# Token gathers one round earlier in the expert stage, and one weight conversion ahead of the first block's copy

## The chip, the cores and the metric

The kernel runs on one core of a Trainium2 chip. The metric is the device time of one execution in microseconds. A core has five engines with an instruction stream each: TensorE (PE in the rows; PEld is its weight load), VectorE (DVE), ScalarE (ACT), GpSimd (POOL) and SyncE (SP), which here only starts transfers. Every stream runs in order: an instruction that waits for a semaphore holds back whatever stands behind it in the same stream. POOL and ACT start transfers too (POOLq, ACTq); the transfers of all three run on the core's 16 DMA engines.

## The reference

Three layers follow each other. An xLSTM-like attention yields 3072 tokens of 320 values. A layer of 8 experts sends each token to the expert with the highest gate logit. A gated feed-forward layer ends it. The change is in the second:

```python
logits = x @ w_gate
e_idx = np.argmax(logits, axis=1)
probs = softmax(logits); gate_w = probs[arange(N), e_idx]
eom = 1 / (1 + exp(-(x @ w_output_gate)))
for e in range(8):
    mask = e_idx == e
    h = relu(x[mask] @ w1[e])          # 320 -> 1024
    out[mask] = gate_w[mask] * eom[mask, e] * (h @ w2[e])   # 1024 -> 320
```

## The kernel before, in words

The program is written by hand, and each engine's stream holds its instructions in the order in which the code issues them. Weights and activations are split into two float16 halves (high and low), so that a product is three matmuls.

**Routing** (`route`) sorts the tokens by expert into blocks of 128 slots, of which 28 always run. `IDX` holds the token of each slot. Behind it come the conversions of the second half of `w2`: `hi` on ACT (L881, 128x1280) and `lo` on DVE (L888). Three raw pieces are parked in the destination of another piece, so the `hi` of piece 4 may write only after the `lo` of piece 6 has read its slot, and that of piece 5 after the `lo` of piece 4. `moe_fetch` starts the gathers of blocks 0 and 1 and turns block 0 on TensorE (`xflip`, L1111), with a copy to `xt` on ACT (L1113).

**The rounds** (`moe`): round `j` runs `up(j)` (16 matmuls of 512 columns, L1143, then ReLU on ACT, the low half on DVE, and two DMA transposes `hT<-h` on SP, L1151) and `down(j-2)` (24 matmuls of 320 columns, L1175). A block's tokens reach `up(j)` in two steps:

- `gather(j)` on POOL (L1095): 128 rows of 1,536 bytes from `XD` in HBM into `xg`. There are two `xg` buffers, so `gather(j+2)` waits until `xpose(j)` has read `xg` of block `j`.
- `xpose(j)` on SP (L1103): a DMA transpose of `xg` into `xt`.

`cgather(j)` on POOL (L1087) fetches the 128 output factors of block `j` into `CG`. `evac(j)` on ACT (L1185) reads them two rounds after the fetch; the first fetch waits for the factors to be written by `coefs`.

**Beside the rounds** 16 jobs (`ffn_jobs`) convert a third of the next layer's weights. A job loads 384 KB on SP into one of four `stg` buffers (L1313), DVE and ACT convert it over four steps, and POOL stores 160 KB into `UWS` (L1341). The load of job `k+4` takes the buffer of job `k`, and so waits on SP until the store of job `k` has landed. `due` says in which round each step runs, and `tick(j, 0)` issues those of part 0 in the middle of `up(j)` and `tick(j, 1)` those of part 1 at the round's end. Loads stand in rounds 2, 3, 4, 5, 6, 8, 9, 10, 11, 12, 14 to 18 and 20, stores in rounds 6 to 10, 12 to 16, 18 to 22 and 24. For three pairs the store of job `k` and the load of job `k+4` fall into the same round: rounds 6, 12 and 18.

SP's order in a round is `xpose(j+1)`, the two `hT` transposes of `up(j)`, the job's load, and then `xpose(j+2)`. In round 23 POOL also starts `fetch(0)`, the first rows of the next layer (L1368), which ACT squares in round 24 (L1383) and TensorE turns at the end of the stage (L1422).

Of the kernel before, what the change touches and what calls it, by code (L numbers as in the profile page):

```python
# [32 lines left out]
NJ = NBLK - 3  # L33
# [41 lines left out]
class Net:  # L75
# [821 lines left out]
    def route(self):  # L897
# [3 lines left out]
        def t(block, n, shape, dt=F32):  # L901

            if block not in blocks:
                if block < 2:
                    b = self.M.tile([128, 2, 4, 128], F16, tag="hT", bufs=5, name="rt").rearrange("p s k c -> p (s k c)")
                else:
                    b = self.M.tile([128, 2, 512], F16, tag="h", bufs=3, name="rt").rearrange("p s f -> p (s f)")
                blocks[block] = [b, 0]
            b, o = blocks[block]
            k = 1  # L910
            for d in shape[1:]:
                k *= d
            w = k * (1 if dt == F16 else 2)
            assert o + w <= 1024
            blocks[block][1] = o + w
            a = b[0 : shape[0], o : o + w]
            a = a if dt == F16 else a.bitcast(dt)
            if len(shape) == 3:
                a = a.rearrange("p (a b) -> p a b", b=shape[2])
            return a  # L920
# [16 lines left out]
        def warm(k):  # L937
            e = P.tile([128, 512], F32, tag="dn", bufs=2, name="warm")
            for _ in range(k):
                nc.tensor.matmul(e, self.id[:, 0:64].bitcast(BF), self.W1[:, 0:512].bitcast(BF), start=True, stop=True)  # L940
# [56 lines left out]
            s = slice(64 * two, 64 * two + 64)  # L997
            nc.vector.tensor_scalar(self.IDX[s], pi[two][s, 0:NBLK], float(NT // 2), None, ALU.add)
        warm(WM[4])
        self.moe_fetch()  # L1000
        ce = t(4, "ce", [1, NBLK, NE], F16)
        nc.vector.scalar_tensor_tensor(
            out=ce, in0=iota[0:1, 0:NBLK].unsqueeze(2).to_broadcast([1, NBLK, NE]), scalar=128.0,
# [8 lines left out]
        w2[0][1]()  # L1012
        w2.append(self.w2load(7))
        w2[4][1]()
        w2[5][0]()
        w2[1][1]()

# [74 lines left out]
    def gather(self, j, xg=None):  # L1092
        if xg is None:
            xg = self.M0.tile([128, 2 * DX], F16, tag="xg", bufs=2, name="xg")
        self.nc.gpsimd.indirect_dma_start(  # L1095
            out=xg, out_offset=None, in_=self.XD,
            in_offset=bass.IndirectOffsetOnAxis(ap=self.IDX[:, j : j + 1], axis=0),
        )
        self.T[j] = dict(xg=xg)

    def xpose(self, j):
        xt = self.M0.tile([128, 6, 128], F16, tag="xt", bufs=2, name="xt")
        self.nc.sync.dma_start_transpose(out=xt, in_=self.T[j]["xg"])  # L1103
        self.T[j]["xt"] = xt
# [7 lines left out]
        xt = self.T[j]["xt"] = self.M0.tile([128, 6, 128], F16, tag="xt", bufs=2, name="xt")  # L1112
        nc.scalar.activation(xt, px, AF.Copy)  # L1113

    def moe_fetch(self):
        self.T, self.X = {}, {}
        self.gather(0)
        self.gather(1)
        self.xflip(0)

    def moe(self):
        nc, M, P = self.nc, self.M, self.P
        gather, xpose = self.gather, self.xpose
# [3 lines left out]
        def up(j, mid=None):  # L1127
            t = T[j]
            e = nc.tensor.value_load(self.EOFF[0:1, j : j + 1], min_val=0, max_val=NE - 1)
            t["e"] = e  # L1130
            o1 = nc.tensor.snap(e * (5 * F1))
            t["hT"] = []
            if j >= NJ:
                own = spare.bitcast(F16)[:, 0:2048].rearrange("p (f s k c) -> p f s k c", f=2, s=2, k=4)
            for f in range(2):
                h = M.tile([128, 2, 512], F16, tag="h", bufs=3, name="h")
                if j < NJ:
                    hT = M.tile([128, 2, 4, 128], F16, tag="hT", bufs=5, name="hT")
                else:
                    hT = own[:, f]  # L1140
                ps = P.tile([128, 512], F32, tag="up", bufs=4, name="ups")
                for n, (kx, kw) in enumerate(UP):
                    nc.tensor.matmul(  # L1143
                        ps, t["xt"][:, kx], self.W1[:, ds(o1 + (kw * F1 + f * 512), 512)],
                        start=(n == 0), stop=(n == 7),
                    )
                nc.scalar.activation(h[:, 0], ps, AF.Relu)  # L1147
                nc.vector.scalar_tensor_tensor(  # L1148
                    out=h[:, 1], in0=ps, scalar=0.0, in1=h[:, 0], op0=ALU.max, op1=ALU.subtract
                )  # L1150
                nc.sync.dma_start_transpose(  # L1151
                    out=hT.rearrange("p s k c -> p (s k) c"), in_=h.rearrange("p s f -> p (s f)")
                )
                t["hT"].append(hT)
                if f == 0 and mid:
                    mid()

        def down(j, mid={}):
            t = T[j]
            oa = nc.tensor.snap(t["e"] * (2 * KA * DM))  # L1160
            ob = nc.tensor.snap(t["e"] * (2 * KB * DM))
            ps = P.tile([128, 512], F32, tag="dn", bufs=2, name="dps")
            n = 0
            for k in range(8):
                if k in mid:
                    mid[k]()
                if k < KA:
                    W, o, kk, nk = self.W2A, oa, k, KA
                else:
                    W, o, kk, nk = self.W2B, ob, k - KA, KB  # L1170
                hi = W[:, ds(o + kk * DM, DM)]
                lo = W[:, ds(o + (nk + kk) * DM, DM)]
                hT = t["hT"][k // 4]
                for l, r in ((0, hi), (1, hi), (0, lo)):
                    nc.tensor.matmul(ps[:, 0:DM], hT[:, l, k % 4], r, start=(n == 0), stop=(n == 23))  # L1175
                    n += 1
            t["dn"] = ps

        def evac(j):
            ps = T[j]["dn"]  # L1180
            if j not in (NJ - 3, NJ - 1):
                y = self.LG.rearrange("p i e -> p (i e)")[:, 0:YC]
            else:
                y = self.M0.tile([128, DX], F32, tag="xg", bufs=2, name="yl")[:, 0:YC]
            nc.scalar.activation(y[:, 0:DM], ps[:, 0:DM], AF.Copy, scale=self.CG[:, j : j + 1])  # L1185
            nc.scalar.activation(y[:, DM:YC].bitcast(I32), self.TOK[:, j : j + 1], AF.Copy)
            nc.scalar.dma_start(self.YD[128 * j : 128 * j + 128], y)
            T.pop(j)
# [11 lines left out]
        def tick(j, part):  # L1200
            for step in due.pop((j - 2, part), []):
                step()
# [3 lines left out]
        gather(3)  # L1206
        gather(4)
        for j in range(NJ):
            if 5 <= j + 2 < NJ:
                gather(j + 2)  # L1210
            if 2 <= j and j + 1 < NJ:
                xpose(j + 1)
            up(j, lambda: tick(j, 0) if j else self.xflip(1))
            if j == 0:
                w2[5][1]()
                w2[2][1]()
                scr = lambda: M.tile([128, 2, 512], F16, tag="h", bufs=3, name="scr").rearrange(
                    "p s f -> p (s f)"
                ).bitcast(F32)
            elif j == 1:  # L1220
                w2[7][0]()
                w2[3][1]()
                w2[7][1]()
                self.weigh(scr())
            elif j == 2:
                down(0)
                self.coefs(scr())
                self.order(scr())
            if j in (8, 10, 12):
                b = NJ + (j - 8) // 2  # L1230
                nc.gpsimd.dma_start(
                    self.YD[128 * b : 128 * b + 128].rearrange("p (s c) -> p s c", s=3),
                    self.zero.unsqueeze(1).to_broadcast([128, 3, YC // 3]),
                )
            if j == 2:
                self.cgather(0)
            if j >= 2:
                self.cgather(j - 1)
            if j > LAG:
                evac(j - LAG - 1)  # L1240
            if j > LAG:
                down(j - LAG)
            if j == FJ[0]:
                self.fetch(0, first=True)
            elif j == FJ[1]:
                self.squares(0, range(4))
                self.norm1(0)
                self.tokens(0)
            elif j == FJ[2]:
                for m in range(4):  # L1250
                    self.norm2(0, m)
            tick(j, 1)
# [428 lines left out]
```

## Time and profile before

| | us |
|---|---|
| three runs of the kernel | 798.79, 808.02, 815.62 |
| median | 808.02 |
| the profiled execution | 794.23 |
| its span, first to last instruction | 792.4 |
| expert stage in that span (first `up` matmul to the last `down`) | 211 to 417 |

The profiled execution is 14 us below the median of the runs shown and 4.6 us below the lowest. Times in the rows are microseconds from the span's start. A timeline row reads: start, duration, engine, line, operation, output<-input, count, and in brackets the idle time of that engine before it with what the profile takes for the releaser. The profile puts a wait for several semaphores down to the one that it saw last; on POOL several rows name DVE where the instruction in the program waits for DMAs alone.

### The profile page before, as it was taken

To read this page: it belongs to the slowest core of one execution; us is meant where nothing else is said; L and a number is where in the kernel's file an instruction comes from. 1 tells how busy PE (TensorE), PEld (TensorE's weight loads), DVE (VectorE), ACT (ScalarE), POOL (GpSimd) and SP (SyncE) were. 2 spreads that over 40 slices of the span, in tenths; PEclk is the share of its full clock that TensorE was granted. 3 is DMA by queue.
4 is the path that set the end of the run, shared out by engine and by line. 5 is a ranking of instruction groups with operands and counts; after the bars stand their busy time and mean duration, and the time that the engine had idled before them with its cause. 6 is when DMAs were issued, how large, how long until landed. Compare 5 with 4: busy or idle time off the path is not lost. (4 is left out here: it accounts for less than half of the span.)

```text
span 792.4 us, 15458 instructions
## 1 busy us (share of the span) xinstructions
PE 758.9 (96%) x5292; PEld 483.0 (61%) x5294; DVE 434.1 (55%) x894; ACT 358.9 (45%) x777; POOL 375.2 (47%) x458
## 2 busy tenths in 40 slices
PE   8899999998798999999989999999999999999997
PEld 8799998986344555555554444444565665644664
DVE  7678988897764646564315776778712112133110
ACT  4578878783532333332436665655422132133110
POOL 2557877883322424234516875765634242233221
PEclk9999999999898999999999999999999999999999
DMA  6587877864669999999965332231131021000000
GB/s 186 169 282 227 278 238 245 268 208 163 206 137 198 212 236 231 238 224 200 191 144 201 99 81 69 76 82 50 51 74 43 26 55 27 26 0 1 13 22 34
DMA packets 131429, 109.21 MB, mean 138 GB/s; under 512 B 104535, under 2 KB 111375, under 8 KB 131353
## 3 DMA queue, kind: packets, MB, share of 16 engines
q1 hardware_dynamic: 120905, 86.64, 43.5%
q0 software_dynamic: 6368, 16.94, 7.4%
q10 hardware_dynamic: 4080, 4.62, 1.8%
q8 instruction: 48, 0.79, 0.4%
q14 instruction: 28, 0.23, 0.1%
HBM read 67.59 MB, written 16.82 MB: 107 GB/s over the span
## 5 line engine op out<-in xcount | busy, mean ns | idle before, releaser
L1518 PE MATMUL gv<-XT,UW 128*128 128x512 f16 x1152 | 249.8, 379 | 1.6 <-DMA XT<-xr 1.6
L1518 PEld LDWEIGHTS <-UW 128*128 128x128 f16 x1152 | 112.6, 98 | 136.9 <-DMA XT<-xr 2.1
L1528 DVE SCALAR_TENSOR_TENSOR u<-th,gv 128x512 f32<-128x512 f32 x72 | 49.4, 686 | 155.6 <-ACT th L1522 153.9
L1534 POOL TENSOR_TENSOR h<-u,h 128x512 f16<-128x512 f32 x72 | 84.8, 1180 | 105.2 <-ACT h L1533 104.8
L1551 PE MATMUL do<-DW,h 128*128 128x320 f16 x864 | 118.5, 299 | 0.9 <-POOL DW L1472 0.9
L1143 PE MATMUL ups<-W,xt 128*128 x448 | 103.7, 385 | 10.2 <-DMA xt<-xg 6.4
L1551 PEld LDWEIGHTS <-h 128*128 128x128 f16 x864 | 84.5, 98 | 34.9 <-issue 1.2
L1533 ACT ACTIVATE h<-u 128x512 f16<-128x512 f32 x72 | 45.3, 629 | 112.7 <-DVE u L1529 112.7
L1147 ACT ACTIVATE h<-ups 128x512 f16<-128x512 f32 x56 | 33.3, 596 | 115.3 <-PE ups L1143 107.8
L1175 PEld LDWEIGHTS <-hT 128*128 128x128 f16 x672 | 65.6, 98 | 31.7 <-issue 2.3
L1148 DVE SCALAR_TENSOR_TENSOR h<-ups,h 128x512 f16<-128x512 f32 x56 | 38.4, 691 | 81.9 <-ACT h L1147 81.5
L1143 PEld LDWEIGHTS <-xt 128*128 128x128 f16 x448 | 44.3, 99 | 62.2 <-DMA xt<-xg 9.4
L1095 POOL DMA_INDIRECT xg<-XD,IDX x28 | 29.7, 1060 | 85.2 <-DMA xt<-xg 38.8
L1556 POOL DMA_INDIRECT out_dram<-os,TKN x24 | 23.5, 977 | 80.3 <-ACT os L1554 76.7
L1529 DVE SCALAR_TENSOR_TENSOR u<-u,gv 128x512 f32<-128x512 f32 x72 | 49.5, 688 | 14.5 <-PE gv L1518 10.2
L485 PE MATMUL S<-QK 104*128 104x128 f32 x384 | 51.6, 278 | 1.8 <-DMA QK<-in_pqk_dram 1.8
L1175 PE MATMUL dps<-W2A,hT 128*128 x336 | 50.5, 299 | 2.1 <-ACTq L1258 2.1
L485 PEld LDWEIGHTS S<-QK 104*128 104x128 f32 x384 | 50.0, 194 | 3.5 <-issue 2.7
L541 PEld LDWEIGHTS Y<-t,D 128*128 128x128 f32 x352 | 49.2, 192 | 3.4
L541 PE MATMUL Y<-t,D 128*128 128x41 f32 x352 | 51.2, 248 | 0.0
L1554 ACT ACTIVATE os<-do 128x320 f32<-128x320 f32 x24 | 10.5, 437 | 88.8 <-PE do L1551 80.7
L1175 PE MATMUL dps<-W2B,hT 128*128 x336 | 50.6, 299 | 0.0
(280 smaller groups left out, 1161.5 us busy)
## 6 DMA issues: line engine op xcount, KB each, us to landing
t<-in_pk_dram SPq DMA_DIRECT2D x22, 484.0 KB
QK<-in_pqk_dram SPq DMA_DIRECT2D x48, 160.0 KB
stg<-in_wu_dram SPq DMA_DIRECT2D x16, 384.0 KB
stg<-in_w_dram SPq DMA_DIRECT2D x9, 640.0 KB
XD<-xr SPq DMA_DIRECT2D x24, 192.0 KB
YD<-LG ACTq DMA_DIRECT2D x26, 160.5 KB
stg<-in_w_dram SPq DMA_DIRECT2D x8, 512.0 KB
wraw<-in_wo_dram SPq DMA_DIRECT2D x12, 320.0 KB
```

What stands on the lines that cost most here:

```text
L485: nc.tensor.matmul(ps[:, i * L : (i + 1) * L], t["kz"][:, j, i], t["t1"][:, i], start=True, stop=True)
L541: nc.tensor.matmul(t["Y"][:, hp, 41 * hf : 41 * hf + 41], t["D"][hf][:, hp * L : (hp + 1) * L], t["vv"][:, 4 * hf + hp], start=False, stop ...
L1143: nc.tensor.matmul(ps, t["xt"][:, kx], self.W1[:, ds(o1 + (kw * F1 + f * 512), 512)], start=(n == 0), stop=(n == 7),)
L1147: nc.scalar.activation(h[:, 0], ps, AF.Relu)
L1148: nc.vector.scalar_tensor_tensor(out=h[:, 1], in0=ps, scalar=0.0, in1=h[:, 0], op0=ALU.max, op1=ALU.subtract)
L1175: nc.tensor.matmul(ps[:, 0:DM], hT[:, l, k % 4], r, start=(n == 0), stop=(n == 23))
L1518: nc.tensor.matmul(ps, UW[:, f, gv, kw], xt[:, :, 3 * hl + kx], start=(a == 0), stop=(a == 7))
L1528: nc.vector.scalar_tensor_tensor(out=u, in0=th, scalar=1.0, in1=pg, op0=ALU.add, op1=ALU.mult)
L1529: nc.vector.scalar_tensor_tensor(out=u, in0=u, scalar=1.0 / (XN * WSC) ** 2, in1=pv, op0=ALU.mult, op1=ALU.mult)
L1533: nc.scalar.activation(hh, u, AF.Copy)
L1534: nc.gpsimd.tensor_tensor(hl, u, hh, ALU.subtract)
L1551: nc.tensor.matmul(ps[:, 0:DM], l[:, s], DW[:, f, w], start=(a == 0), stop=(a == 3 * NF - 1))
```

## The change

Three edits. `moe_fetch` is dissolved: its two gathers stay where they were, and its `xflip(0)` moves behind the `hi` of piece 4, so that ACT converts this piece before it copies block 0. In `moe` the line that gathers now stands behind `xpose(j+1)`, and it gathers block `j+3`, no more `j+2`.

```diff
@@ route
         warm(WM[4])
-        self.moe_fetch()
+        self.T, self.X = {}, {}
+        self.gather(0)
+        self.gather(1)
         ce = t(4, "ce", [1, NBLK, NE], F16)
...
         w2[6][1]()
         w2[4][0]()
         w2[0][1]()
         w2.append(self.w2load(7))
         w2[4][1]()
+        self.xflip(0)
         w2[5][0]()
         w2[1][1]()
...
-    def moe_fetch(self):
-        self.T, self.X = {}, {}
-        self.gather(0)
-        self.gather(1)
-        self.xflip(0)
@@ moe
         for j in range(NJ):
-            if 5 <= j + 2 < NJ:
-                gather(j + 2)
             if 2 <= j and j + 1 < NJ:
                 xpose(j + 1)
+            if 5 <= j + 3 < NJ:
+                gather(j + 3)
             up(j, lambda: tick(j, 0) if j else self.xflip(1))
```

**POOL, rounds 0 to 6.** `xg` is a gather (numbers grow with the block; the first row is block 4), `CG` a fetch of factors, `UWS` a job's store. Lines below the change have other numbers in the new program. Before:

```order
L1095 DMA xg_3202<-XD_81,IDX_69 128x768
L1087 DMA CG_67<-CD_83,IDX_69 128x1 x2
L1095 DMA xg_3393<-XD_81,IDX_69 128x768
L1087 DMA CG_67<-CD_83,IDX_69 128x1
L1095 DMA xg_3465<-XD_81,IDX_69 128x768
L1087 DMA CG_67<-CD_83,IDX_69 128x1
L1095 DMA xg_3542<-XD_81,IDX_69 128x768
L1087 DMA CG_67<-CD_83,IDX_69 128x1
L1095 DMA xg_3625<-XD_81,IDX_69 128x768
L1341 DMA UWS_87<-stg_3391 128x640
```

Now:

```order
L1098 DMA xg_3202<-XD_81,IDX_69 128x768
L1098 DMA xg_3312<-XD_81,IDX_69 128x768
L1090 DMA CG_67<-CD_83,IDX_69 128x1 x2
L1098 DMA xg_3397<-XD_81,IDX_69 128x768
L1090 DMA CG_67<-CD_83,IDX_69 128x1
L1098 DMA xg_3469<-XD_81,IDX_69 128x768
L1090 DMA CG_67<-CD_83,IDX_69 128x1
L1098 DMA xg_3546<-XD_81,IDX_69 128x768
L1090 DMA CG_67<-CD_83,IDX_69 128x1
L1098 DMA xg_3629<-XD_81,IDX_69 128x768
L1338 DMA UWS_87<-stg_3393 128x640
```

The gather of block 5 now stands ahead of the first two fetches of factors. From there on every fetch and every store has one more gather ahead of it: the store of job 0 (round 6) stood behind the gather of block 8, and stands behind that of block 9.

**ACT at the end of routing and in the first block.** `W2B` is a conversion of L881, `xt<-xpx` the copy of a block, `h<-ups` a ReLU. Before:

```order
L881 ACTIVATE W2B<-W2B 128x1280
L1113 ACTIVATE xt<-xpx 128x768
L881 ACTIVATE W2B<-W2B 128x1280 x2
L1147 ACTIVATE h<-ups 128x512
L1113 ACTIVATE xt<-xpx 128x768
```

Now:

```order
L881 ACTIVATE W2B<-W2B 128x1280 x2
L1116 ACTIVATE xt<-xpx 128x768
L881 ACTIVATE W2B<-W2B 128x1280
L1144 ACTIVATE h<-ups 128x512
L1116 ACTIVATE xt<-xpx 128x768
```

One of the two conversions that stood between the two copies now stands ahead of both. The streams of TensorE, DVE and SP keep their order.

## Rows read from the trace of the kernel before

**Rows 1.** The page, 40 slices of the span: granted TensorE clock, DMA share.

```profile
PEclk9999999999898999999999999999999999999999
DMA  6587877864669999999965332231131021000000
```

**Rows 2.** Waits of TensorE, 205 to 415: total us, times, longest.

```profile
PE ups L1143 <- DMA xt<-xg: 6.4, 5, 3.8
PE dps L1175 <- ACTq L1258: 2.1, 1, 2.1
```

**Rows 3.** Waits of POOL and of SP's queue, same stretch and columns.

```profile
POOL xg L1095 <- DMA xt<-xg: 38.8, 7, 7.4
...
SPq L1103 <- DMA xg<-XD,IDX: 1.5, 2, 0.9
```

**Rows 4.** Timeline, end of routing and first block.

```profile
210.11 0.81 ACT L1113 ACTIVATE xt<-xpx 128x768 f16<-128x768 f16 x1 [3.77 <-PE xpx L1111]
...
210.82 1.26 ACT L881 ACTIVATE W2B<-W2B 128x1280 f16<-128x1280 f32 x1
...
213.64 1.27 ACT L881 ACTIVATE W2B<-W2B 128x1280 f16<-128x1280 f32 x1 [1.56 <-DVE W2B L888]
...
216.24 7.07 PE L1143 MATMUL ups<-W,xt 128*128 x32 [1.21 <-DVE h L1148]
```

**Rows 5.** Timeline of rounds 3 to 5: transposes of blocks 4 and 5.

```profile
231.43 1.23 SPq L1103 DMA_TRANSPOSE xt<-xg  x1
...
234.55 0.95 POOL L1095 DMA_INDIRECT xg<-XD,IDX  x1 [0.30 <-issue]
...
235.39 3.61 PE L1143 MATMUL ups<-W,xt 128*128 x16 [0.25 <-DMA xt<-xg]
...
239.17 1.22 SPq L1103 DMA_TRANSPOSE xt<-xg  x1
...
246.03 6.10 PE L1143 MATMUL ups<-W,xt 128*128 x16 [3.77 <-DMA xt<-xg]
```

**Rows 6.** Stretches: busy us of the engines, granted clock, DMA share, GB/s.

```profile
238.00:244.00 6.00, 4.27 (x29) 2.62 (x27) 3.45 (x7) 1.22 (x3) 0.94 (x1) 1.00 1.04 217
244.30:251.10 6.80, 5.07 (x12) 1.88 (x13) 0.83 (x2) 1.46 (x4) 1.88 (x2) 0.50 0.84 198
...
408.00:415.00 7.00, 5.40 (x48) 4.02 (x48) 0.00 (x0) 1.67 (x6) 0.00 (x0) 1.00 0.60 177
```

**Rows 7.** Timeline of POOL: stores of rounds 6, 7 and 13, gather of round 7.

```profile
254.95 0.61 POOL L1341 DMA_DIRECT2D UWS<-stg  x1 [2.31 <-issue]
...
261.85 0.95 POOL L1095 DMA_INDIRECT xg<-XD,IDX  x1 [5.01 <-DVE stg L1335]
262.79 0.60 POOL L1341 DMA_DIRECT2D UWS<-stg  x1
...
304.54 0.59 POOL L1341 DMA_DIRECT2D UWS<-stg  x1
```

**Rows 8.** Timeline of SP's queue: loads and transposes of rounds 6 and 12.

```profile
262.04 1.42 SPq L1313 DMA_DIRECT2D stg<-in_wu_dram  x1
263.55 1.36 SPq L1103 DMA_TRANSPOSE xt<-xg  x1
...
303.65 0.53 SPq L1313 DMA_DIRECT2D stg<-in_wu_dram  x1
304.27 1.22 SPq L1103 DMA_TRANSPOSE xt<-xg  x1
```

**Rows 9.** Line L1341, the 16 stores into `UWS`, from issue to landing.

```profile
DMA to landing us min/median/max: 2.6/4.5/6.6
```

**Rows 10.** Timeline of TensorE: first matmuls of rounds 8 and 14.

```profile
269.41 3.61 PE L1143 MATMUL ups<-W,xt 128*128 x16 [0.59 <-DVE stg L1301]
...
311.49 3.61 PE L1143 MATMUL ups<-W,xt 128*128 x16 [0.92 <-DMA xt<-xg]
```

**Rows 11.** Timeline of rounds 23 to 27: last row fetch, first square, first flip.

```profile
377.56 0.97 POOL L1368 DMA_INDIRECT stg<-YD,RSLOT  x1 [0.17 <-issue]
...
385.64 0.44 ACT L1383 ACTIVATE junk<-stg 128x320 f32<-128x320 f32 x1 [0.40 <-ACT LG L1186]
...
412.55 0.50 PE L1422 MATMUL fpx<-stg 128*128 128x128 f16 x6
```

## The prediction

> **What bounds the kernel now.** I read the page's slices first. TensorE holds its full clock nearly everywhere, and in slices 10 and 12 it loses a little [rows 1]. In slices 12 to 19, the rounds of the expert stage, the DMA line is at its top. So two things are full there, and a late transfer becomes a wait of TensorE. The waits of TensorE in this stage say how much there is to win: 6.4 us for `xt<-xg` in five waits, one of 3.8 among them [rows 2]. A gather earlier helps only if transposes wait for gathers. SP's waits answer that: `xpose` (L1103) waited for `xg` twice, 1.5 us together, while the gathers (L1095) waited 38.8 us for `xt<-xg`, that is for a transpose to have read the buffer [rows 3]. **Except at the start of the stage, the gathers wait for transposes and not the other way round.** A gather that its buffer holds doesn't go out sooner because it stands sooner in POOL's stream; it only stands longer in front of what is behind it.
>
> **The change, part by part.** The sum is made on the profiled execution (794.2 us, 14 us under the median of the runs shown); I add its difference to the median.
>
> 1. *The conversion ahead of the first copy.* ACT sat idle for 3.77 us before it copied block 0, and converted piece 4 right after, 1.26 us with no wait of its own. Piece 5 then waited 1.56 us more for DVE's `lo` of piece 4, ran until 214.9, and so the copy of block 1 came late and `up(1)` waited 1.21 us [rows 4]. With piece 4 in the idle time, `lo` of piece 4 and `hi` of piece 5 move up by over a microsecond, and the copy of block 1 is in time. Bounds: -1.2 (the wait goes, and all of it reaches round 3) and +1.3 (piece 4's data comes so late that the conversion delays the copy by itself). That it ran with no wait right after the copy puts the data ahead of that. I take -0.8, two thirds of the wait, because DVE's other `lo` steps stand behind ReLU and can't all move.
>
> 2. *The gather of block 5.* Before, it stood behind the first two fetches of factors, which wait for the factors, and left at 234.55; `xpose(5)` left at 239.17 and TensorE got block 5 at 246.03 after a gap of 3.77 us [rows 5]. Now it stands ahead of those fetches, and its buffer is free once `xpose(3)` has landed. SP's wait of up to 0.9 us [rows 3] goes; I count 0.7. Its 192 KB also leave the stretch in which `xpose(5)` is on the way: at the 217 GB/s of that stretch [rows 6] some 0.9 us. So the gap falls from 3.77 to about 2.2. After the old gap the clock was at half (granted 0.50, 1.2 GHz) and 16 matmuls took 6.10 us where they take 3.61 [rows 5, 6], so 2.5 us more. A gap of 2.1 us at the end of the stage left the clock at 1.00 [rows 2, 6], which is nearer to 2.2 than 3.77 is. I take -1.6 and -2.5, together -4.1; bounds 0 and -6.3.
>
> 3. *Three stores behind one more gather.* In round 6 the store of job 0 left at 254.95. Now the gather of block 9 stands ahead of it. That gather left at 261.85 and the next store at 262.79, right behind it [rows 7]; its buffer can't be free sooner, so job 0's store takes this slot, 7.8 us later. (The row names a DVE step as the releaser; the instruction waits for DMAs alone.) Most stores can bear this, since the load that needs their buffer comes a round later. In rounds 6, 12 and 18 it comes in the same round, at 262.04 in round 6 [rows 8], before the store has even left. SP then waits at the load, and `xpose(8)` stands behind it, with the `hT` transposes of round 7. A store takes 2.6 to 6.6 us to land, median 4.5 [rows 9]. The transpose leaves 0.6 us after its load [rows 8], and a transpose behind a load took from 4.0 us to the first matmul (231.43 to 235.39 [rows 5], with little in SP's queue) to 7.2 (304.27 to 311.49 [rows 8, 10], with a full one). I take 5.0, nearer to the short one, because SP has issued nothing for over 4 us. Round 8 would start at 262.79 + 4.5 + 0.6 + 5.0 = 272.9 and not at 269.41, +3.5. For the load of round 12 the slot is 304.54 [rows 7], and round 14 starts at 314.6 and not at 311.49, +3.1. Round 18 repeats it; I take the mean, 3.3. Together +9.9. Bounds: the shortest of each (2.6 + 0.6 + 4.0) gives +0.6 and +0.2 and about 0.4, +1.2; the longest (6.6 + 0.6 + 7.2) gives 7.8, 7.4 and 7.6, +22.8.
>
>    The Trainium skill, "DMA: Bandwidth & Descriptors", section "Anatomy of one DMA — SWDGE (gpsimd) path", puts a transfer from this path at about 2.0 us plus its bytes over 436 GB/s, which is 2.4 us for such a store. By that the three waits would shrink by 2.1 us each and the sum of this step to 3.6. The rows have 4.5 in the middle, with the DMA engines full, and the sum goes by them.
>
> 4. *The clock after those gaps.* With the 0.59 and 0.92 us that rounds 8 and 14 waited already [rows 10], the three gaps come to about 4 us each, as long as the one that halved the clock [rows 5, 6]. Each halving costs 2.5 us. Taking two of three: +5.0; bounds 0 and +7.5.
>
> 5. *Edits at nothing.* The fetches of factors go out a gather later, by up to a round; `evac` reads them two rounds after, and a round is 7.0 us here ((311.49 - 269.41) / 6 [rows 10]). The other twelve loads that reuse a buffer wait for a store of an earlier round; if one of them lands at 6.6 instead of 4.5, 2 us could be lost. `fetch(0)` stands behind the gather of block 26 instead of 25, and its last row fetch moves from 377.56 by up to a round; the squares at 385.64 then end a few microseconds late and delay a ReLU of round 25 by about one, which TensorE doesn't read for two rounds, and the flips come at 412.55 only [rows 11]. Without this cover it would cost a round's 7 us.
>
> Sum: -0.8 - 4.1 + 9.9 + 5.0 = **+10.0 us**, 804 on the profiled execution and 808.0 + 10.0 = **818 us** on the median.
>
> **Rivals.**
>
> *The stores land in time, and the stage gets faster.* The mechanism is the slot of step 3: from the store's issue to the first matmul there are 269.41 - 262.79 = 6.6 us in round 6 and 7.0 in round 12 [rows 7, 10]. If landing, load and transpose together take about 7 us, near their shortest sum of 7.2, step 3 costs about 1 and step 4 nothing. What is left is -0.8 - 4.1 + 1.2 = -3.7: 804 us. For it: with SP held, the DMA engines have less to do, and a transpose without a load ahead may land sooner than any row here shows. Against it: POOL's own gather and fetch go out beside the store, and medians give 10.1. The 2.4 us for a store of the Trainium skill's page ("DMA: Bandwidth & Descriptors", the same section) would lead to this side.
>
> *Early gathers pay as a rule.* If the gathers did move, because POOL's idle time before them is DVE's as the rows say and not the buffer's, the waits of 6.4 us and the halved clock's 2.5 us would go and step 3 not arise: -0.8 - 6.4 - 2.5 = -9.7, 798 us. The 38.8 us of [rows 3] speak against it. The Trainium skill, "DMA: Bandwidth & Descriptors", section "Rules for kernel authors", says to issue a DMA early and to wait for it late; by that rule the time would come out on this side, and these rows bear it out only where the buffer is free.
>
> *Everything lands late.* Step 3 near its upper bound (about +18), three halvings (+7.5), and 4.9 gained: +20 us, 828 us. The row for it is 304.27 to 311.49, a transpose that took 7.2 us with no help from this change.
>
> *The change does nothing that shows.* Steps 2 and 3 cancel within 3 us: 808 us.
>
> **How the numbers follow.** Chances: forecast (from +4 to +16) 0.55, stores in time 0.14, early gathers pay 0.05, late landings 0.16, nothing that shows 0.10. The predicted time is the likeliest case, 818. The range takes in the stores in time at its low end and late landings at its high end, with some microseconds for the spread of the runs shown (798.79 to 815.62): 802 to 832. Two per cent, about what a measurement of this kernel can tell from no change, are 16.2 us: slower than 824.2 are the late landings and the upper edge of the forecast with a high median, 0.22; faster than 791.9 would need the early gathers and a low median, 0.03; the rest, 0.75, lies within.
>
> **What would show it.** Right: SP's load (L1310 then) waits about 4 us in rounds 6, 12 and 18, and TensorE waits 3 to 5 us for `xt<-xg` at the start of rounds 8, 14 and 20, with the granted clock at 0.5 behind some of them; the gap at round 5 is near 2 us and that at round 1 gone; the gathers from round 6 on leave at the same point of a round as before. Wrong: loads that leave on time, gathers a round sooner in time, or a gap at round 5 that stays at 3.8. If the three gaps come without a halved clock, step 4 falls and 813 is nearer.

## The result and the profile after

The changed kernel takes 807.19 us (median of 21 runs, 801.91 to 819.85), the kernel before 804.02 in as many runs beside it. The ratio is 1.0058, 95% interval 1.0035 to 1.0082: **4.7 us slower (2.8 to 6.6)**. The ratio leaves out, on both sides, the runs over 1.5% above the fastest one, so it differs a little from the 3.2 us between the medians. The forecast was +10.0 us and 818 us: the sign is right, the size about twice too large. Of the 10.8 us between 818 and 807.19, 4.0 lie in the base (808.02 from three runs, 804.02 from 21).

The profiled execution after took 813.31 us. That it lies 19 us above the one of before is for the greater part not the change: the page shows the clock below nine tenths in slices 6, 8 and 10 (counted from 0, as in the prediction), which lie ahead of the experts (they start at 225 us, in slice 11).

```profile
PEclk9999998959799999999999999999999999999999
DMA  6587877755459999999877332231221011000000
```

So only the expert stage is compared, from its first `up` matmul to the first matmul of the next layer: 206.5 us before, 211.2 after. The second profiles of the two kernels (`e6_before`, `e5_again` below) have 210.9 and 214.7: the difference is alike, but one kernel's stage varies as much from one execution to the next. The waits of that stage, of TensorE, POOL and SP's queue (total us, times, longest), which answer to [rows 2, 3]:

```profile
PE ups L1140 <- DMA xt<-xg: 9.6, 7, 2.9
...
POOL xg L1098 <- DMA xt<-xg: 54.9, 9, 14.0
POOL xg L1098 <- DMA hT<-h: 24.3, 4, 8.0
...
SPq L1310 <- DMA UWS<-stg: 11.4, 5, 4.8
SPq L1106 <- DMA xg<-XD,IDX: 1.2, 1, 1.2
```

Three things are to be seen. SP now waits for stores, 11.4 us in all; in the profile of before it did not (1.2 us, once, in `e6_before`). The gathers stand longer for their buffer (38.8 us before, 54.9 now behind the same transfer; their whole idle time is 85.2 and 115.5), as the prediction's first paragraph has it, and the gather of block 9 leaves at the same point, 0.4 us ahead of the first matmul of round 7 (0.1 before). And TensorE waits 3.2 us longer for `xt`.

Rounds 6 and 12 on the timeline: the store on POOL, the load that needs its buffer and the transpose on SP, and the first matmuls two rounds on (start, duration, engine and line; in brackets TensorE's wait):

```profile
271.28 0.61 POOL L1338 DMA_DIRECT2D UWS<-stg  x1
...
274.58 0.33 SPq L1310 DMA_DIRECT2D stg<-in_wu_dram  x1
275.00 1.95 SPq L1106 DMA_TRANSPOSE xt<-xg  x1
...
280.15 5.08 PE L1140 MATMUL ups<-W,xt 128*128 x15 [2.56 <-DMA xt<-xg]
...
316.57 0.59 POOL L1338 DMA_DIRECT2D UWS<-stg  x1
...
320.44 0.33 SPq L1310 DMA_DIRECT2D stg<-in_wu_dram  x1
320.87 1.37 SPq L1106 DMA_TRANSPOSE xt<-xg  x1
...
325.47 4.89 PE L1140 MATMUL ups<-W,xt 128*128 x16 [2.85 <-DMA xt<-xg]
```

This is step 3, link by link. The load leaves 3.30 and 3.87 us behind the store (3.43 in round 18), the transpose 0.42 later, and the matmuls 5.15 and 4.60 later (5.37). The forecast had 4.5, 0.6 and 5.0. Together 8.9 to 9.2 us instead of 10.1. TensorE waits 2.56, 2.85 and 1.98 us before rounds 8, 14 and 20, where it waited 0.59, 0.92 and 0.51 [rows 10 for the first two]: 5.4 us more, not 9.9.

Behind the first two of these gaps the clock is at half (granted 0.50, 1.2 GHz), behind the third it is not (1.00). A stretch behind the gap before round 8 (busy us of PE, PEld, DVE, ACT, POOL with counts, granted clock, DMA share, GB/s):

```profile
280.40:283.60 3.20, 3.20 (x9) 1.21 (x8) 0.00 (x0) 0.00 (x0) 2.51 (x3) 0.50 0.94 215
```

Rounds 8 and 14 then last 1.69 and 1.28 us longer than the 6.71 of a round without a wait. That is 3.0 us for step 4, not 5.0.

Round 5, which answers to [rows 5]: its transpose leaves at 251.49, and the first matmul runs at 257.29 with no wait and at full clock. Before, there were 3.77 us of wait and a halved clock.

```profile
251.49 1.33 SPq L1106 DMA_TRANSPOSE xt<-xg  x1
...
257.29 2.97 PE L1140 MATMUL ups<-W,xt 128*128 x13
```

The first block, which answers to [rows 4]: `up(1)` waits nearly as long as before (1.05 us, 1.21 before).

```profile
229.42 0.81 ACT L1116 ACTIVATE xt<-xpx 128x768 f16<-128x768 f16 x1 [1.52 <-PE ups L1140]
...
230.38 1.89 PE L1140 MATMUL ups<-W,xt 128*128 x8 [1.05 <-ACT xt L1116]
```

The copy of block 1 waits for matmuls of `up(0)`, not for ACT's conversions: there are two `xt` buffers, one holds block 2 by then, and the copy takes that of block 0, so it can't begin before `up(0)` has ended.

At the end of the stage, in round 24, ACT stands still for 5.24 us in front of a ReLU, and rounds 25 and 26 start 0.96 and 1.61 us late. That is 2.6 of the 4.8 us by which this profile's stage is longer, and the second profile of the change does not have it (0.8 us there, below). "Remote" means that the trace has no releaser.

```profile
399.65 0.60 ACT L1144 ACTIVATE h<-ups 128x512 f16<-128x512 f32 x1 [4.54 <-PE ups L1140]
...
405.48 0.60 ACT L1144 ACTIVATE h<-ups 128x512 f16<-128x512 f32 x1 [5.24 <-remote]
```

### The profile page after: what moved, and what is told of

It reads as the page before. It is cut to its first block, busy times and chain, and to the rows that moved or that the text cites. A ratio compares the mean times of both kernels' runs of the same rounds, so it can differ in the third digit from the quotient of the medians.

```text
span 811.5 us, 15452 instructions
## 1 busy us (share of the span) xinstructions
PE 770.2 (95%) x5292; PEld 492.3 (61%) x5294; DVE 434.8 (54%) x894; ACT 359.3 (44%) x777; POOL 373.9 (46%) x458
## 5 line engine op out<-in xcount | busy, mean ns | idle before, releaser
L1098 POOL DMA_INDIRECT xg<-XD,IDX x28 | 27.6, 986 | 115.5 <-DMA xt<-xg 54.9
L485 PE MATMUL S<-QK 104*128 104x128 f32 x384 | 55.4, 291 | 3.4 <-DMA QK<-in_pqk_dram 3.4
L485 PEld LDWEIGHTS S<-QK 104*128 104x128 f32 x384 | 54.1, 208 | 5.2 <-issue 4.2
L541 PEld LDWEIGHTS Y<-t,D 128*128 128x128 f32 x352 | 53.2, 206 | 4.0 <-issue 0.9
L541 PE MATMUL Y<-t,D 128*128 128x41 f32 x352 | 54.4, 259 | 0.0
L1519 ACT ACTIVATE th<-gv 128x512 f32<-128x512 f32 x72 | 42.2, 586 | 17.4 <-PE gv L1515 17.4
```

The source lines that it names most:

```text
L485: nc.tensor.matmul(ps[:, i * L : (i + 1) * L], t["kz"][:, j, i], t["t1"][:, i], start=True, stop=True)
L541: nc.tensor.matmul(t["Y"][:, hp, 41 * hf : 41 * hf + 41], t["D"][hf][:, hp * L : (hp + 1) * L], t["vv"][:, 4 * hf + hp], start=False, stop ...
L1519: nc.scalar.activation(th, pg, AF.Tanh, scale=0.5 / (XN * WSC))
```

## The experiments

All ratios are to the kernel before, run beside them. **Store theory:** the loss is what the three held loads do to the transposes behind them. **Rivals:** the loss lies in the other rounds, through POOL's other order; or there is a gain at round 5 of the forecast's size, which hides part of a larger loss.

**The three held loads alone** (`e2_stores`, the kernel before with only this):

```diff
-            if 5 <= j + 2 < NJ:
+            if 5 <= j + 2 < NJ and j not in (7, 13, 19):
                 gather(j + 2)
             if 2 <= j and j + 1 < NJ:
                 xpose(j + 1)
+            if j in (6, 12, 18):
+                gather(j + 3)
```

> The kernel before, with the gathers of blocks 9, 15 and 21 one round sooner, in rounds 6, 12 and 18, so that just the three stores whose buffer the same round's load wants stand behind a gather that waits for its buffer. Store theory: SP waits at those three loads, gaps at rounds 8, 14 and 20 grow by 1.5 to 2 us each (5.4 in the changed kernel's profile) and a halved clock adds up to 3; 5 to 9 us slower, ratio 1.006 to 1.011. As my forecast had it, 10 us for the gaps and 5 for the clock: 1.019. Rival (the stores' place is of no weight): 0.998 to 1.002.

Ratio 1.0111 (1.0053 to 1.0168), +8.9 us (4.2 to 13.4). Its waits of SP and TensorE in the stage:

```profile
SPq L1315 <- DMA UWS<-stg: 14.4, 3, 5.8
```

```profile
PE ups L1143 <- DMA xt<-xg: 15.8, 7, 4.4
```

The held loads alone make the kernel slower, by 8.9 us against the 14.9 of steps 3 and 4. Whether that is more than the whole change costs the intervals don't tell.

**The change with the store ahead of the gather** (`e3_swap`): the gather stands behind `up(j)`, in whose middle the store is issued.

```diff
-            if 5 <= j + 3 < NJ:
-                gather(j + 3)
             up(j, lambda: tick(j, 0) if j else self.xflip(1))
+            if 5 <= j + 3 < NJ:
+                gather(j + 3)
```

> The changed kernel, with the gather of block j+3 behind up(j) in place of in front of it, so that a job's store in the middle of up(j) stands ahead of the gather again; the fetches of factors stay behind it. Store theory: SP waits at no load, the gaps at rounds 8, 14 and 20 are under 1 us as in the kernel before, and the gain at round 5 stays: 5 us faster than the kernel before, ratio 0.992 to 0.996. Rival (late fetches of factors, or gathers at other times, cost what the change lost): as the changed kernel, 1.003 to 1.008.

Ratio 1.0006 (0.9964 to 1.0048).

```profile
SPq L1310 <- DMA UWS<-stg: 1.1, 1, 1.1
```

No load of rounds 6, 12 and 18 waits as in the change (1.1 us in all), and no loss is left that the interval (-2.9 to +3.8 us) could show. The gain of 5 us that I had expected from round 5 did not come: that round still waits 2.06 us.

**The conversion alone** (`e4_conv`, the kernel before with the edits in `route`).

```diff
-        self.moe_fetch()
+        self.T, self.X = {}, {}
+        self.gather(0)
+        self.gather(1)
...
         w2[4][1]()
+        self.xflip(0)
```

> The kernel before with the conversion of piece 4 ahead of the copy of block 0 alone. As forecast: the wait of 1.2 us at block 1 goes and 0.8 us come of it. From the changed kernel's trace, where this wait is 1.05 us: the copy of block 1 takes the buffer of block 0 and can't start before up(0) has ended, so 0.2 us at most. Ratio 0.998 to 1.001 either way; what tells them apart is the wait of TensorE at block 1, 0 to 0.4 us or 1.0 to 1.2.

Ratio 1.0002 (0.9961 to 1.0042), and the wait of `up(1)` is again 1.05. From the first `up` matmul to that of round 3 it is 17.0 to 17.1 us in the eight profiles with this edit and 17.2 to 17.3 in the nine without: step 1 is worth 0.2 us at most.

**Step 2.** The gather of block 5 alone, in round 2 (`e1_early5`, and profiled a second time, `e8_early5`), and the gathers of blocks 5 to 7 as in the change, with the old order from round 6 (`e7_start`). The edits on the kernel before, of `e1_early5` and of `e7_start`:

```diff
-            if 5 <= j + 2 < NJ:
+            if 6 <= j + 2 < NJ:
                 gather(j + 2)
...
+            if j == 2:
+                gather(5)
```

```diff
-            if 5 <= j + 2 < NJ:
+            if 8 <= j + 2 < NJ:
                 gather(j + 2)
...
+            if 2 <= j <= 4:
+                gather(j + 3)
```

> The kernel before, with one gather moved: that of block 5 stands ahead of the first two fetches of factors (round 2) and not behind them. All other gathers keep their round. Store theory (the change loses time only where SP is held at a load by a late store): the gap at round 5 and its halved clock go (6.4 us in the changed kernel's profile), round 4 gives 1.0 us back, no gap of 2 us or more at rounds 8, 14 and 20; 5 us faster, ratio 0.992 to 0.996. Rival (gathers at other times slow the transposes on the full DMA engines, wherever they go): the gap only moves from round 5 to a neighbour, ratio 0.998 to 1.003.

> The kernel with the gather of block 5 alone moved, for a second profile. If the early gather of block 5 doesn't touch the gap at round 5: 3 us or more again. Rival (the first profile caught a DMA stall): under 2 us.

> The gathers of blocks 5, 6 and 7 a round sooner, as in the changed kernel, and from round 5 on the order of the kernel before, so that no store stands behind one more gather. If the changed kernel's start makes the gain at round 5 (POOL held at the gather of block 7 keeps its transfers out of the stretch in which the transpose of block 5 runs): gap at round 5 under 1 us, no halved clock, 1 us back at round 4, no gaps over 2.2 us at rounds 8 and 20; ratio 0.992 to 0.996 to the kernel before. Rival (the gap at round 5 comes and goes by itself): a gap of 2 us or more, ratio 0.997 to 1.002.

`e1_early5`: ratio 0.9966 (0.9925 to 1.0008). `e7_start`: 0.9989 (0.9950 to 1.0029). Round 5 of `e7_start`, whose stream on POOL up to there is that of the change:

```profile
237.72 1.14 SPq L1315 DMA_DIRECT2D stg<-in_wu_dram  x1
238.97 1.22 SPq L1103 DMA_TRANSPOSE xt<-xg  x1
...
246.97 5.30 PE L1143 MATMUL ups<-W,xt 128*128 x16 [4.50 <-DMA xt<-xg]
```

The gap is 4.50 us, longer than before. `e1_early5` has 3.66 there, `e8_early5`, the same program, 2.12. So the same stream on POOL gives a gap of another length in each execution. The 0 us in the profile after can't be read as the change's gain.

**Both kernels profiled again** (`e5_again` the change, `e6_before` the kernel before).

> The changed kernel once more, for a second profile. If its profile shows the change and not one execution: SP waits for stores at the loads of rounds 6, 12 and 18 (11 to 15 us in all), gaps of 2 to 3.5 us at rounds 8, 14 and 20, under 1 us at round 5; rounds 25 and 26 take 6.7 to 7.7 us each. Rival (the 5 us in which ACT stood still in round 24 of the first profile belong to the change): round 25 or 26 takes over 7.5 us again, with a ReLU of round 24 late by 4 us or more.

> The kernel before once more, for a second profile, to see how far the gap at round 5 varies by itself. If that gap is made by the order of POOL's stream: 3.3 to 4.2 us again, with a halved clock. Rival (it depends on when the DMA engines happen to stall): outside of that, 2 to 3 or over 4.3.

The change: SP waits for stores again, three times and 9.6 us in all, and rounds 8, 14 and 20 wait 2.51, 0.66 and 2.33 us. The gap at round 5 is 2.74, not under 1. Two squares of the next layer wait for their rows on ACT:

```profile
SPq L1310 <- DMA UWS<-stg: 9.6, 3, 4.7
```

```profile
ACT junk L1380 <- DMA stg<-YD,RSLOT: 3.9, 2, 3.4
```

The kernel before has a gap of 4.55 at round 5 and a halved clock, and its squares wait for no row.

**The change without the three held loads** (`e9_three`, and profiled again, `e15_three_again`): only the gathers of blocks 9, 15 and 21 go back behind the store.

```diff
-            if 5 <= j + 3 < NJ:
+            if 5 <= j + 3 < NJ and j not in (6, 12, 18):
                 gather(j + 3)
             up(j, lambda: tick(j, 0) if j else self.xflip(1))
+            if j in (6, 12, 18):
+                gather(j + 3)
```

> The changed kernel, but in rounds 6, 12 and 18 alone the gather stands behind the middle of the round again, and so behind the store; all other gathers keep the place of the change. If the three held loads are the whole loss (store theory): SP waits for stores under 2 us in sum and not 11.4, the gaps at rounds 8, 14 and 20 are under 1.5 us each, and the ratio to the kernel before is 0.997 to 1.001 (799 to 803 where before has 802). Rival, the loss lies elsewhere too (later fetches of factors, later rows of the next layer): the ratio stays at 1.003 to 1.006.

> The changed kernel with the three stores ahead of the gather, profiled a second time. If its gaps at rounds 10, 14, 18 and 20 (2.8, 1.8, 1.6, 2.8 us in the first profile) follow from its order, POOL's two gathers within 3 to 5 us of each other and a transpose that then takes over 8 us, they come again at the same rounds, over 1.5 us each. If they come by chance, as the gap at round 5 does, they stand at other rounds.

Ratio 1.0049 (1.0013 to 1.0086). No load waits for a store, as expected, but by this ratio a loss stays, and the store theory as I had put it would fall: the held loads would not be all of it. The ratio is a weak witness, though, since the medians of all runs, 804.09 and 804.55 for the kernel before, show no loss. Round 8 of `e9_three` and the matmuls of round 10:

```profile
267.63 0.95 POOL L1098 DMA_INDIRECT xg<-XD,IDX  x1 [5.79 <-DVE stg L1300]
268.59 0.59 POOL L1340 DMA_DIRECT2D UWS<-stg  x1
...
270.75 1.29 POOL L1098 DMA_INDIRECT xg<-XD,IDX  x1 [0.30 <-issue]
272.04 0.59 POOL L1340 DMA_DIRECT2D UWS<-stg  x1
...
274.77 2.19 SPq L1106 DMA_TRANSPOSE xt<-xg  x1
...
283.38 0.81 PE L1140 MATMUL ups<-W,xt 128*128 x3 [2.79 <-DMA xt<-xg]
```

Two gathers and two stores leave within 4.4 us, a transpose that leaves right behind them needs 8.6 us to the matmul, and TensorE waits 2.79 us. The second profile has its large gaps at rounds 12 and 14 (3.02, 1.75), not at rounds 10, 14, 18 and 20 as the first: only round 14 comes again. So where the gaps stand does not follow from this order.

**The transposes ahead of the loads.** The transposes of blocks are what TensorE waits for, and a load of 384 KB leaves on SP right ahead of each of them. `e10_xf_after` (the change) and `e11_xf_before` (the kernel before) turn this round from block 4 on; `e12_xf_early5` adds the gather of block 5 in round 2 to the second.

```diff
-            if 2 <= j and j + 1 < NJ:
-                xpose(j + 1)
+            if 2 == j:
+                xpose(3)
...
+            if 2 <= j and j + 2 < NJ:
+                xpose(j + 2)
             tick(j, 1)
```

> The changed kernel, but on SP the transpose of the next block stands ahead of the job's load of the round and no more behind it (from block 4 on). Store theory: the load still waits about 4 us for its store in rounds 6, 12 and 18, 9 to 12 us in sum, but no block's transpose stands behind it, so the gaps at rounds 8, 14 and 20 fall under 1 us and the ratio to the kernel before is 0.994 to 1.000. Rival: the held load holds the hT transposes of the next round, and the wait turns up in front of a down: ratio 1.003 to 1.006.

> The kernel before with only this: on SP the transpose of the next block stands ahead of the job's load of the round (from block 4 on). If the gap at round 5 (2.7 to 4.5 us in the profiles of kernels with gathers in four different orders) comes from the 384 KB of the load that is issued 1 to 2 us ahead of the transpose, the gap falls under 2 us, the clock is not halved behind it, and the ratio is 0.992 to 0.997. Rival, the transposes are late because the DMA engines are full whatever stands in front: gap 2.5 to 4.5 as before, ratio 0.998 to 1.002.

> The kernel before with two edits: the gather of block 5 in round 2, behind the transpose of block 3 (as in the changed kernel, the other gathers as before), and on SP each block's transpose ahead of the job's load of the round. If both help: ratio 0.988 to 0.995. If only the order on SP helps: the same as the kernel with that edit alone. If neither: 0.996 to 1.002.

Ratios: `e10_xf_after` 0.9923 (0.9873 to 0.9973), `e11_xf_before` 0.9893 (0.9843 to 0.9943), `e12_xf_early5` 0.9868 (0.9826 to 0.9911). The last two are 8.6 and 10.6 us faster than the kernel before and beat both kernels; whether the gather of block 5 adds to it the intervals don't tell. (Nor do `e10_xf_after` and `e11_xf_before` differ by more than theirs.) The waits in `e10_xf_after`, of SP and then TensorE:

```profile
SPq L1312 <- DMA UWS<-stg: 10.7, 3, 4.2
```

```profile
PE ups L1140 <- DMA xt<-xg: 2.2, 2, 1.6
```

The loads are held as long as in the change (10.7 us against 11.4), and TensorE hardly waits for `xt` (1.6 us at round 14 is the longest). So **a held load costs mainly through the transpose that stands behind it.** The store and the load of round 6 there, and the transpose between:

```profile
257.26 0.61 POOL L1340 DMA_DIRECT2D UWS<-stg  x1
257.76 1.36 SPq L1106 DMA_TRANSPOSE xt<-xg  x1
263.42 0.33 SPq L1312 DMA_DIRECT2D stg<-in_wu_dram  x1
```

A transpose leaves within 0.5 us of the store, and the load follows 6.2 us behind the store (5.4 and 4.4 the other two times), where the change has 3.3 to 3.9 with no block's transpose between. Round 5 of `e11_xf_before`:

```profile
242.34 1.21 SPq L1103 DMA_TRANSPOSE xt<-xg  x1
243.60 0.57 SPq L1315 DMA_DIRECT2D stg<-in_wu_dram  x1
...
247.06 3.61 PE L1143 MATMUL ups<-W,xt 128*128 x16 [0.64 <-DVE stg L1300]
```

From the transpose to the matmul it is 4.7 us here, and 6.9 behind the load [rows 5] or 8.0 (`e7_start`). In the three kernels with this turn the gap at round 5 is 0.2 to 0.6 us: what sets it is the load in front of the transpose more than the gather behind the factors.

**The same turn in rounds 6, 12 and 18 alone** (`e13_xf3_after` on the change, `e14_xf3_before` on the kernel before).

```diff
-            if 2 <= j and j + 1 < NJ:
+            if 2 <= j and j + 1 < NJ and j not in (7, 13, 19):
                 xpose(j + 1)
...
+            if j in (6, 12, 18):
+                xpose(j + 2)
             tick(j, 1)
```

> The changed kernel, but in rounds 6, 12 and 18 alone the transpose of the next block stands ahead of the job's load on SP; POOL's stream is that of the change. The three loads still wait for their stores, 9 to 12 us in sum. If the transposes behind these three loads are the loss (store theory): gaps at rounds 8, 14 and 20 under 1 us, ratio to the kernel before 0.997 to 1.002, and as fast as the kernel before with the same three transposes moved. Rival, the loss is spread over all rounds through POOL's other order: gaps of 1.5 to 3 us come at other rounds instead, and the ratio stays at 1.003 to 1.007.

> The kernel before with the same three transposes (rounds 6, 12, 18) ahead of the load. Here no load waits for a store, so both theories expect little: the small gaps at rounds 8, 14 and 20 (0.6, 0.9, 0.5 us in its profile) shrink, ratio 0.996 to 1.000.

`e13_xf3_after`: 1.0034 (0.9992 to 1.0076). `e14_xf3_before`: 0.9993 (0.9950 to 1.0036). Round 6 of the first:

```profile
261.93 1.85 SPq L1106 DMA_TRANSPOSE xt<-xg  x1
...
262.24 0.61 POOL L1340 DMA_DIRECT2D UWS<-stg  x1
265.66 0.33 SPq L1312 DMA_DIRECT2D stg<-in_wu_dram  x1
...
268.75 3.62 PE L1140 MATMUL ups<-W,xt 128*128 x16
```

The load still leaves 3.42 us behind its store, the transpose 3.7 us ahead of the load, and round 8 starts with no wait; so do rounds 14 and 20. The three gaps were the work of the transposes behind the held loads. (SP's waits for stores sum to 3.4 us, less than the 9 to 12 expected, since the load now comes to its place later.) What may be left of the loss (the interval of the ratio takes in 1) would lie in other rounds.

**Where the waits stand, kernel by kernel.** From the first `up` matmul of each round on the timelines, I sum by how much a round starts later than 6.71 us behind the one before (us; a halved clock shows in the next round; before again is `e6_before`, after again `e5_again`):

```
                   rounds 4-7   8,14,20   others 9-23   sum 4-23   24-27
before                 6.8        2.5         2.0         11.3       0.0
before again           7.8        2.8         3.5         14.2       0.0
e4_conv                4.9        4.3         2.9         12.1       0.2
e1_early5              7.0        3.0         1.1         11.1       0.0
e8_early5              2.9        3.5         2.4          8.9       0.0
e7_start               6.9        2.6         3.7         13.1       0.0
e14_xf3_before         6.0        0.0         2.4          8.4       3.1*
e2_stores              6.2        9.7         4.9         20.7       0.0
after                  1.4        7.9         4.4         13.7       2.6*
after again            3.2        6.0         8.2         17.4       0.8
e3_swap                2.5        3.8         4.4         10.6       1.1
e9_three               1.2        5.5         6.4         13.1       2.3*
e15_three_again        3.2        2.4         6.5         12.1       3.1*
e13_xf3_after          6.8        0.0         5.6         12.3       3.7*
e10_xf_after           0.9        2.4         1.3          4.7       3.5*
e11_xf_before          1.9        1.7         0.0          3.7       2.5*
e12_xf_early5          0.8        0.8         0.9          2.6       2.2*
```

The sum over rounds 4 to 23 follows the held loads. It is 17.3 on the mean of the three profiles in which a transpose stands behind a held load (`e2_stores`, after, after again), 11.3 in the seven with the old order from round 6 on (the first seven rows), and 12.0 in the four of the change in which no block's transpose does (`e3_swap`, `e9_three`, `e15_three_again`, `e13_xf3_after`). Single profiles overlap: after has 13.7, before again 14.2.

The star marks the profiles in which ACT stands still for 4 to 10 us at the end with the releaser "remote". They are of both gather orders. In each of them most records of DMA landings are missing from 2 us before the first row fetch to 8 us behind it, and between 210 and 420 us there are 2,426 to 2,613 such records; the others have 3,189 to 3,334 and no such hole. Whether the kernel halts there or the recording makes it halt stays open, so rounds 24 to 27 are not in the sum.

## Why the prediction was right and wrong

- *What bounds the stage, and that gathers wait for transposes:* right. In the change they stand longer in front of POOL's stores and move nothing in most rounds.
- *Step 3, the mechanism:* right, shown from both sides: alone it costs 8.9 us, and with the transposes out of the load's way rounds 8, 14 and 20 start on time.
- ***Steps 3 and 4, the size:* this is where the prediction failed.** +14.9 was forecast; the profile has 5.4 + 3.0 = 8.4, the run with these loads alone 8.9 (4.2 to 13.4). Two terms were mis-sized.
  - The store's landing. I took the median of all 16 stores [rows 9], 4.5 us, and these three took 3.3 to 3.9 (3.4 to 4.2 in `e5_again` and `e2_stores`). The likely reason is that SP, standing at the load, sends next to nothing meanwhile; in `e10_xf_after`, where a block's transpose leaves beside the store, it is 4.4 to 6.2. I had said this of the transpose and not of the store. With 0.4 for 0.6 from the load to the transpose, the chain is 0.9 to 1.2 us shorter each time, 3.3 us in all, and as it ends in a wait, all of that came off the wait. Most of the other 1.2 us of step 3 is that the store of round 18 left 0.9 us earlier in its round than the slot it had in the trace of before. The Trainium skill, "DMA: Bandwidth & Descriptors", section "Anatomy of one DMA — SWDGE (gpsimd) path", gives about 2.4 us by the estimate in the prediction; these stores lie between it and the median.
  - The price of a halved clock. It followed two gaps of three, as forecast, but cost 1.7 and 1.3 us and not 2.5 each: the stretch at half clock was 3.4 us long both times, that of [rows 6] 6.8.
- *Step 2, -4.1:* not established. Over the profiles, the gap at round 5 is 2.7 to 4.6 us with the old order (five profiles) and 0 to 4.5 with the gathers of the change (after, after again, e7, e9, e13, e15; mean 2.5). That mean is near the 2.2 of the forecast, but the runs of `e7_start` (-0.9 us, -4.0 to +2.3) show no gain. Its cause was mistaken: the load ahead of the transpose sets this gap more than the gather does.
- *Step 1, -0.8:* wrong, it is 0.2 at most. I had looked at what ACT does and not at which buffer the copy writes.
- *Step 5, nothing:* about right for the squares' rows (0.8 us in after again). POOL's other order does more than that: the other rounds hold 4.4 to 8.2 us of waits in the five profiles of the change and its variants without the full turn on SP, and 1.1 to 3.7 in the seven with the old order in those rounds (of the 4.4 of after, 3.0 are the halved clock of step 4). Rounds 4 to 7 hold less in turn, and that the two together are a loss is not shown.
- *The sum:* with 8.4 for 14.9 it is +3.5; with steps 1 and 2 at nothing as well, since no run shows their gains, +8.4. The measured 4.7 (2.8 to 6.6) lies between. So the right sign is the work of step 3, and the steps' sizes are not settled further.
- *The rivals:* the stores did not land in time, and early gathers did not pay as a rule. The gather of block 5, whose buffer came free ahead of its old place in the stream, left 17.4 us behind the first `up` matmul and not 23.5; the others waited for their buffers. The Trainium skill, "DMA: Bandwidth & Descriptors", section "Rules for kernel authors", says to issue early and wait late; no run here shows a gain from it in this stage.

**Open:** whether anything of the loss remains when no block's transpose stands behind a held load. The ratio of `e9_three` says 3.9 us (1.0 to 6.9), the medians of its runs show none, and the sums of rounds 4 to 23 little (12.0 against 11.3); `e13_xf3_after` (1.0034) and `e3_swap` (1.0006) have intervals that take in 1 and overlap with that of `e9_three`. What the order of gathers does to the waits is seen only in the profiles: fewer in rounds 4 to 7 (2.6 us on the mean), more in the others. It may be that a held load also thins the traffic of its round, so that freeing it moves the wait to a transpose in another round; `e9_three` shows one such bunch, and no run isolates it.

## What to carry to other kernels

Before an issue is moved earlier in an in-order stream, ask what its buffer waits for: if it can't leave sooner, the move only delays what stands behind it, and the price is paid where another queue waits for that. Put the transfer that the bound engine waits for ahead of bulk loads in the same queue; in `e10_xf_after` loads that were over 10 us late in all cost little, with no block's transpose behind them. A gap that one profile shows is worth counting on only after a second profile of the same program shows it too.

## What was not expected of the hardware

The same program gives gaps of 3.66 and 2.12 us (`e1_early5`, `e8_early5`) and of 0 and 2.74 us (the change) at the same round. A DMA transpose took 4.7 us to the first matmul with a load of 384 KB issued 1.3 us behind it, and 6.9 to 8.0 with one issued 1.3 to 2.1 us ahead of it ([rows 5] and `e7_start`; the load of before left at 237.03): the order of two issues on one queue, 2 us apart, goes with over 2 us at the end, though 16 DMA engines share the work. It is no fixed price: behind a load, a transpose also took 4.0 us (block 4 in [rows 5]) and 4.6 to 5.4 (the held ones of the change), and one ahead of its load took 8.5 (block 14 in `e10_xf_after`).
